# First weight rows in one tile, early sums in pairs of 64 columns, a shorter split, unit 3 transposed by TensorE, and a new order in an attention-and-MoE kernel

## The chip, the cores and the metric

The kernel runs on one core of a Trainium2 chip. The metric is the device time in microseconds (us), the median of three runs. The core has five engines with instruction streams of their own: PE (TensorE; the weight loads are shown apart as PEld), ACT (ScalarE), DVE (VectorE), POOL (GpSimd) and SP (SyncE, which here only issues DMAs). Each stream runs in the order in which it was written, and semaphores hold an instruction until what it needs is there.

## The reference

Attention over 4 batches, 8 heads, 768 positions and 64 values a head. Heads 0, 2 and 6 see all earlier positions; the other five see the last 64 positions and the first four (the sinks). Then a gated layer turns each of the 3072 tokens of 512 values into 2048 and back.

```
scores = where(mask, q @ k.T / 8, -1e9)              # per batch and head
a      = softmax(scores);  attn = a @ v
x      = attn, heads side by side                    # 3072 x 512
h      = x @ w_in                                    # 512 x 2048
out    = (h * sigmoid(beta * h)) @ w_out             # 2048 x 512
```

## The kernel before, in words

**Units.** The work is cut into eight units of 384 queries: unit n is half u = n % 2 of batch b = n // 2. Each goes through the same stages. q and k are loaded, cast to bf16 and turned, so that the head dimension lies on partitions (tiles `QK`). TensorE makes scores in rounds (`scores`, written S in what follows; unit, head pair, round), ACT takes their exponentials (`exps`, tile `es`), DVE multiplies by masks (`masks`). TensorE sums them per query and head (`sums`, `sums_d`) and multiplies them with v (`pv`, two halves). The reciprocals of the sums are spread over partitions, and the products with them are `xT`. The layer then takes 16 blocks of 128 columns of `w_in`: `mm1` is four matmuls of 384 columns, `swish_a` (ACT) a tanh into tile `t`, `swish_b` (DVE) the gate into `gT`. `mm2` multiplies `gT` with `w_out`: three output blocks of 16 matmuls, then a copy by ACT or DVE and a store.

**Early and late units.** Units 0 and 1 (`RD = 2`) have a way of their own: `sums` adds by matmuls with a column selector `esel`, 128 queries to a group of 32 partitions; `recips` takes reciprocals of 96x128; `split` cuts them into a high and a low bf16 part on other partitions of `hl` by one cast and three operations; `spread` is one matmul for each quarter of `xT`; `hold` copies pv's result out of PSUM, and `norm_held` multiplies. The later units send their sums through memory (`sums_turn`, `spread_w`, `spread_r`, all on SP's queue). Units below `TD = 3` are loaded by head pair (`load_qk`, 192 KB) and turned by TensorE (`transposes`, six 128x128 transposes for a head pair, then `qk_copy`); the others are loaded by blocks of 128 positions (`load_block`), cast on POOL and turned by three DMA transposes on SP's queue (`turn_block`).

**Weights.** `w_in` and `w_out` come in four transfers of 1 MB each into tile `wf`, of which there are three buffers. `cast_w_in` and `cast_w_out` cast them on POOL. The first 128 rows of `w_in` belong to heads 1 and 0, which `xT` holds in that order, so `swap_w_in` casts these rows by two instructions of 64 rows that change places.

**The order.** Nothing follows from loops. `add` (line 127 ff.) lists each step with its engine or a choice of engines, what it needs and gives, and which ring of buffers it takes from; `SEQUENCE` names the order of all 1104 steps and `CHOICE` the engine where there is a choice. Every engine gets its steps in the order of `SEQUENCE`. `fill` puts idle matmuls in front of unit 0's steps on PE. PSUM has four single banks (`b`) and two double ones (`sp`), so a score round waits until an earlier one has been read by ACT.

In the order of before, PE has these steps just ahead of the first mm1 of unit 0: unit 0's sums and pv, unit 1's S 3 0, unit 0's four spreads, unit 1's S 3 1, two transpositions, S 3 2 and S 1 0. SP issues q of unit 0 and part of unit 1 first, then v of unit 0, then weights; the four transfers of `w_out` are issued between 28 and 41 us, with the loads of q and k of unit 2 partly behind them. Unit 3's q and k are loaded at 45 to 55 us, and its three turns are issued at 60.6 us. The mm2 of unit 0 begins between mm1 blocks 7 and 8 of unit 1.

Of the kernel before, what the change touches and what calls it, by code (L numbers as in the profile page):

```python
# [8 lines left out]
F32 = mybir.dt.float32  # L9
BF16 = mybir.dt.bfloat16  # L10
# [14 lines left out]
TD = 3  # L25
# [65 lines left out]
]  # L91
CHOICE = (
    "addddddggggdaaaaaaadgddaagggggaddggddaaaaaaddaaddaaadddggagggdggagggadgdgaaaadagaadadaaaaddaaddadaaa"
    "aaada"
# [24 lines left out]
class _Plan:  # L119
# [10 lines left out]
    def add(self, eng, cost, f, needs=(), gives=(), take=(), drop=(), dma=0.0, mode=None, port=False, begun=()):  # L130
# [4 lines left out]
        self.ops.append((0, len(self.ops), dict(alts), (lambda e: f()) if one else f, tuple(needs), tuple(gives),  # L135
                         tuple(take), tuple(drop), dma, mode, port, tuple(begun)))

    def run(self):
# [4 lines left out]
        bus, lock = 2.0, 0.0  # L143
# [3 lines left out]
        for o in (self.ops[i] for i in SEQUENCE):  # L147
            _, i, costs, f, needs, gives, take, drop, dma, md, port, begun = o
# [22 lines left out]
            if dma:  # L171
                bus = max(bus, t + (0.5 if dma > 0.2 else cost)) + dma
                end = bus + (1.9 if dma > 0.2 else 3.2)
                now[e] = max(now[e], bus - 2.8)
# [15 lines left out]
def kernel(  # L190
# [27 lines left out]
    RINGS = dict(  # L218
        q2f=5, k2f=5, vf=3, wf=3, c=4, vb=2, vs=2, xT=2, gT=2, t=2, osb=3, R=1, sc=1, rec=1, hl=1, VE=2,
        KP1=1, KP2=1, KP3=1,  # L220
        sp=2, b=4, **{f"es{pi}_{u}": 1 for pi in range(NP) for u in range(2)})

# [1023 lines left out]
```

## Time and profile before

| what | value |
|---|---|
| median of 3 runs (lowest, highest) | 237.85 us (237.45, 237.98) |
| span of the profiled execution | 236.2 us (its own time is not listed apart; the median is 1.65 us above the span) |
| busy: PE, DVE, ACT, POOL | 224.1, 148.9, 145.3, 94.1 us |
| chain that ended last | PE 72%, DMA 18%, POOL 3%, the rest under 3% each |
| moved by DMA | 43.14 MB |
| granted TensorE clock | mean 0.978; half in the stretch from 13.0 to 23.3 us |

Nearly all lines of the program are recorded under one helper (L113), so the profile is read by tiles: `b<-xT,w_in` is mm1, `b<-w_out,gT` is mm2, `t` and `gT` are the two halves of the gate, `sp<-QK` are scores, `sp<-es,vb` is pv, `b<-ident,c` are transpositions by TensorE, `QK<-c` is a turn by DMA. Times in the timeline are from the first instruction; the second column is how long the group of merged rows lasted.

### The profile page before, as it was taken

The numbers are of one execution on the slowest core, as the hardware profiler recorded it, in microseconds if no ns is written. First come the engines' busy times: TensorE is split into PE (matmuls) and PEld (weight loads), VectorE is DVE, ScalarE is ACT, GpSimd is POOL, SyncE is SP. The second block draws the span as 40 slices with busy tenths as digits, with TensorE's granted clock in tenths as the row PEclk, the third lists the DMA queues.
The fourth block names the chain that finished last, engine by engine and source line by source line (L and its number), as shares of the span: only waits on it lengthen the run. The fifth ranks groups of instructions, "written<-read, shape, count | busy, mean of one in ns | idle before, by whom it ended". The sixth has DMA issues, their size and how long they took to land.

```text
span 236.2 us, 5989 instructions
## 1 busy us (share of the span) xinstructions
PE 224.1 (95%) x2337; PEld 128.3 (54%) x2359; DVE 148.9 (63%) x340; ACT 145.3 (62%) x247; POOL 94.1 (40%) x220
## 2 busy tenths in 40 slices
PE   8789889999999997999999999999999999999994
PEld 8447457555535454546556555655465554655553
DVE  4579699888736667397667557855478466344600
ACT  3889987866836457824996498247459452154720
POOL 5344787676265551596550238195212000000000
PEclk9965999999999999999999999999999999999999
DMA  6989999999999999999959899975570025210312
GB/s 196 312 203 375 346 260 318 319 269 230 184 213 231 222 219 195 199 157 287 223 144 200 127 262 223 189 132 126 130 175 3 2 92 142 89 44 3 133 44 89
DMA packets 91980, 43.14 MB, mean 183 GB/s; under 512 B 75808, under 2 KB 84720, under 8 KB 91952
## 3 DMA queue, kind: packets, MB, share of 16 engines
q1 hardware_dynamic: 90864, 41.98, 76.8%
q10 hardware_dynamic: 1088, 0.79, 1.1%
q8 instruction: 18, 0.29, 0.6%
q14 instruction: 10, 0.08, 0.1%
HBM read 32.38 MB, written 6.37 MB: 164 GB/s over the span
## 4 chain that ended last, share of the span: by engine, by line
PE 72%; DMA 18%; POOL 3%; SPq 2%; issue 2%; DVE 1%; ACT 0%; DVEq 0%; ACTq 0%
PE b L113 63%; PE sp L113 9%; DMA wf<-in_moe_w_out_dram 7%; DMA vf<-in_v_dram 7%; DMA q2f<-in_q_dram 2%; SPq L113 2%; DMA QK<-c 2%; POOL w_out L113 1%; POOL c L113 1%; DVE xT L113 1%; DVE c L113 0%; POOL vb L113 0%; ACT t L113 0%; DVE mask_s L113 0%; ACT osb L113 0%
## 5 line engine op out<-in xcount | busy, mean ns | idle before, releaser
L113 DVE SCALAR_TENSOR_TENSOR gT<-t,b 128x384 bf16<-128x384 f32 x128 | 69.2, 551 | 42.8 <-ACT t L113 39.0
L113 ACT ACTIVATE t<-b,beta_h 128x384 f32<-128x384 f32 x128 | 72.9, 583 | 36.1 <-PE b L113 30.2
L113 PE MATMUL b<-xT,w_in 128*128 128x384 bf16 x512 | 91.6, 326 | 0.9 <-DVE gT L113 0.6
L113 PE MATMUL b<-w_out,gT 128*128 128x512 bf16 (+1 forms) x378 | 87.7, 370 | 1.7 <-issue 1.0
L113 PEld LDWEIGHTS <-w_in 128*128 128x128 bf16 x512 | 48.6, 98 | 37.1 <-issue 2.5
L113 PEld LDWEIGHTS <-gT 128*128 128x128 bf16 x400 | 37.6, 98 | 39.2 <-issue 1.9
L113 ACT ACTIVATE es<-sp 128x768 bf16<-128x768 f32 (+3 forms) x64 | 49.1, 806 | 12.1 <-PE sp L113 11.8
L113 POOL CAST c<-wf 128x256 bf16<-128x256 f32 x60 | 22.6, 419 | 16.9 <-DMA wf<-in_k_dram 15.9
L113 ACT ACTIVATE osb<-b 128x512 f32<-128x512 f32 (+1 forms) x17 | 9.9, 585 | 25.9 <-PE b L113 20.0
L113 POOL COPY KP<-QK 128x64 bf16<-128x64 bf16 (+5 forms) x47 | 12.8, 320 | 27.8 <-DMA QK<-c 25.7
L113 PE MATMUL sp<-QK 64*64 64x64 bf16 (+6 forms) x402 | 19.8, 242 | 3.0 <-DMA QK<-c 1.2
L113 POOL CAST vb<-wf 128x512 bf16<-128x512 f32 x18 | 11.6, 667 | 16.2 <-DMA wf<-in_v_dram 16.2
L113 PEld LDWEIGHTS <-QK 64*64 64x64 bf16 (+1 forms) x402 | 10.4, 107 | 13.7 <-issue 11.5
L113 DVE TENSOR_TENSOR xT<-sp,R 128x768 bf16<-128x768 f32 (+3 forms) x18 | 11.6, 686 | 7.5 <-PE sp L113 7.4
L113 PE MATMUL sp<-es,vb 128*64 128x64 bf16 (+3 forms) x243 | 14.7, 245 | 0.0
L113 DVE TENSOR_TENSOR es<-es,mask_s 128x800 bf16<-128x800 bf16 (+5 forms) x24 | 13.1, 557 | 1.0 <-ACT es L113 1.0
L113 POOL COPY vs<-vb 64x1536 bf16<-64x1536 bf16 (+2 forms) x10 | 12.6, 1271 | 0.4
L113 PEld LDWEIGHTS <-vb 128*64 128x64 bf16 x243 | 12.4, 116 | 0.5
L113 DVE TENSOR_TENSOR es<-es,mask_c 128x256 bf16<-128x256 bf16 (+2 forms) x32 | 10.7, 348 | 2.7 <-ACT es L113 2.4
L113 POOL CAST w_in<-wf 128x384 bf16<-128x384 f32 (+1 forms) x20 | 10.1, 537 | 5.7 <-DMA wf<-in_moe_w_in_dram 5.4
L113 POOL CAST w_out<-wf 128x512 bf16<-128x512 f32 x16 | 10.1, 670 | 4.8 <-DMA wf<-in_moe_w_out_dram 4.8
L113 ACT COPY QK<-b 128x384 bf16<-128x384 bf16 (+1 forms) x16 | 8.3, 548 | 5.0 <-PE b L113 2.8
(92 smaller groups left out, 169.8 us busy)
## 6 DMA issues: line engine op xcount, KB each, us to landing
out_dram<-osb SPq DMA_DIRECT2D x23, 256.0 KB
wf<-in_v_dram SPq DMA_DIRECT2D x18, 256.0 KB
wf<-in_moe_w_in_dram SPq DMA_DIRECT2D x4, 1024.0 KB
wf<-in_moe_w_out_dram SPq DMA_DIRECT2D x4, 1024.0 KB
wf<-in_q_dram SPq DMA_DIRECT2D x15, 256.0 KB
wf<-in_k_dram SPq DMA_DIRECT2D x15, 256.0 KB
R<-rd SPq DMA_DIRECT2D x9, 384.0 KB
q2f<-in_q_dram SPq DMA_DIRECT2D x12, 192.0 KB
```

What stands on the lines that cost most here:

```text
L113: ins = f(*a, **k)
```

## The change

It has five parts and a new order.

- **First rows of w_in.** `load_w0` loads the first 128 rows into one tile, 64 rows by 1024 columns at a time, with the two halves of 64 rows already changed over. `cast_w0` casts 128x256 at a time, 8 times. `load_w_in` loads the other three blocks of 128 rows (768 KB instead of 1 MB). The `wf` ring keeps its three buffers and has five such tiles before `w_out` instead of four.
- **Sums of units 0 and 1.** They are cut into three parts, `SUMS = [(0,), (1, 2), (3,)]` by head pair, each issued when its pairs are ready. A matmul has 64 columns instead of 128, so there are twice as many (70 and 126 instead of 35 and 63), and the sums lie on 96x64 instead of 96x128.
- **Reciprocals and split.** The reciprocal is of 96x64; the split is a cast of 96x64, one operation of 96x64 and one bf16 product of 96x384.
- **Unit 3.** `TD = 4`: its q and k are loaded by head pair, cast by eight POOL instructions, and turned by 24 transposes of TensorE and four copies of 128x768 by ACT or DVE, instead of by blocks and three DMA transposes.
- **First mm1 blocks.** Blocks 0 and 1 of unit 0 are issued quarter by quarter, each quarter needing only its own part of `xT`.
- **Order.** `SEQUENCE` and `CHOICE` are new, and some of the costs that `add` is given. SP now issues unit 0's v right behind six loads of q and k; `w_out` comes behind all q and k of unit 2. PE's steps ahead of the first mm1 no longer hold unit 1's S 3 1, S 3 2, S 1 0 and three of its transpositions. All 32 mm1 blocks of units 0 and 1 come before the first mm2. Unit 4's three turns are issued before unit 3's sums go through memory; in the kernel before, two of them came behind.

```diff
-TD = 3
+TD = 4
...
-    def const_esel():
-        pool.memset(esel, 0.0)
-        for j in range(8):
-            pool.memset(esel[:, j, :, j:j + 1], 1.0)
+    def const_two():
+        pool.memset(two, 0.0)
+        pool.memset(two[:, 31:40:8], 1.0)
...
+    def load_w0(half, r):
+        if (half, r) == (0, 0):
+            wst["0"] = stg.tile([128, 2048], F32, name="wf", bufs=RINGS["wf"])
+        c = slice(half * d_ff // 2, (half + 1) * d_ff // 2)
+        sp.dma_start(out=wst["0"][r:r + D, c], in_=moe_w_in[D - r:2 * D - r, c])
...
-    def swap_w_in(s, half, eng):
-        f = wst["i", s][:, 0, half * FS:(half + 1) * FS]
-        for r in (0, D):
-            cast(eng, w_in_sb[2 * s + half][r:r + D, 0, :], f[D - r:2 * D - r, :])
+    def cast_w0(s, eng):
+        cast(eng, w_in_sb[s][:, 0, :], wst["0"][:, s * FS:(s + 1) * FS])
...
+    SUMS = [(0,), (1, 2), (3,)]
...
+            for s in range(2):
+                a = j * 128 + s * W
+                for h in heads:
+                    e8 = two[:, 31 - 16 * s - XH.index(h):63 - 16 * s - XH.index(h)]
...
+                    pe.matmul(x.sm[32 * j:32 * j + 32, 0:W], l, e, start=(part == r == 0),
+                              stop=(part == len(SUMS) - 1 and r == len(byj[j]) - 1))
...
-        dve.reciprocal(x.sm[0:96, 0:128], x.sm[0:96, 0:128])
+        dve.reciprocal(x.sm[0:96, 0:W], x.sm[0:96, 0:W])
...
-        for j in range(TU):
-            r = slice(32 * j, 32 * j + 32)
-            dve.scalar_tensor_tensor(out=hl[r, j * 128:(j + 1) * 128], in0=hi[r], scalar=low[r], in1=rec[r],
-                                     op0=MULT, op1=ADD)
+        dve.scalar_tensor_tensor(out=lo, in0=hi, scalar=low[0:96], in1=rec, op0=MULT, op1=ADD)
+        dve.tensor_mul(x.hl, lo.unsqueeze(1).to_broadcast([96, CK, W]), blk)
...
+        if n == 0 and s < 2:
+            for t in range(NP):
+                add("pe", 0.163, lambda t=t: mm1(x, s, [t]), needs=[("xT", n, t)] + ([("h", n, s, t - 1)] if t else needs if s != 1 else needs[:2] + [("h", n, 0, 0)]),
+                    gives=[("h", n, s, t)] + ([("h", n, s)] if t == NP - 1 else []), take=[] if t else take)
```

More of the change, by code (lines that the diff above doesn't have):

```diff
@@ L128, in __init__, with add @@
         self.same = {}
-    def add(self, eng, cost, f, needs=(), gives=(), take=(), drop=(), dma=0.0, mode=None, port=False, begun=()):
+    def add(self, eng, cost, f, needs=(), gives=(), take=(), drop=(), dma=0.0, mode=None, port=False, begun=(), lat=None):
         needs = dict.fromkeys(m for n in needs for m in self.same.get(n, [n]))
@@ L135, in add @@
         self.ops.append((0, len(self.ops), dict(alts), (lambda e: f()) if one else f, tuple(needs), tuple(gives),
-                         tuple(take), tuple(drop), dma, mode, port, tuple(begun)))
+                         tuple(take), tuple(drop), dma, mode, port, tuple(begun),
+                         lat or (1.9 if dma > 0.2 else 3.2)))
     def run(self):
@@ L147, in run @@
         for o in (self.ops[i] for i in SEQUENCE):
-            _, i, costs, f, needs, gives, take, drop, dma, md, port, begun = o
+            _, i, costs, f, needs, gives, take, drop, dma, md, port, begun, lat = o
             e = {"a": "act", "d": "dve", "g": "pool"}[choice[i]] if i in choice else list(costs)[0]
@@ L172, in run @@
                 bus = max(bus, t + (0.5 if dma > 0.2 else cost)) + dma
-                end = bus + (1.9 if dma > 0.2 else 3.2)
+                end = bus + lat
                 now[e] = max(now[e], bus - 2.8)
@@ L218 @@
     RINGS = dict(
-        q2f=5, k2f=5, vf=3, wf=3, c=4, vb=2, vs=2, xT=2, gT=2, t=2, osb=3, R=1, sc=1, rec=1, hl=1, VE=2,
+        q2f=5, k2f=5, vf=3, wf=3, c=4, vb=2, vs=2, xT=2, gT=2, t=2, osb=3, R=1, sc=1, rec=1, VE=2,
         KP1=1, KP2=1, KP3=1,
@@ L724, in sink_from, with sums @@
         return 2 * W if u == 0 else 0
-    def sums(x):
-        sm = bank((x.n, "s"))
-        if x.n == 0:
-            fill(sm[:, 0:128])
+    SUMS = [(0,), (1, 2), (3,)]
+    def sums(x, part):
+        if part == 0:
+            x.sm = bank((x.n, "s"))
+            if x.n == 0:
+                fill(x.sm[:, 0:128])
         byj = [[] for _ in range(TU)]
+        heads = [h for pi in SUMS[part] for h in PAIRS[pi]]
         for j in range(TU):
-            if j * 128 >= sink_from(x.u):
-                byj[j].append((esel_k.rearrange("p a b -> p (a b)"), x.esk[0:96, j * 128:(j + 1) * 128]))
-        for hpos, h in enumerate(XH):
-            e8 = esel[:, hpos, :, :].rearrange("p a b -> p (a b)")
-            for j in range(TU):
-                if RETR[h]:
-                    byj[j] += [(e8, e[:, j * 128 - q0:j * 128 - q0 + 128])
-                               for (kb, q0, n, e) in x.work[h] if q0 <= j * 128 < q0 + n]
-                else:
-                    byj[j].append((e8, x.work[h][:, j * 128:(j + 1) * 128]))
+            for s in range(2):
+                a = j * 128 + s * W
+                for h in heads:
+                    e8 = two[:, 31 - 16 * s - XH.index(h):63 - 16 * s - XH.index(h)]
+                    if RETR[h]:
+                        byj[j] += [(e8, e[:, a - q0:a - q0 + W]) for (kb, q0, n, e) in x.work[h] if q0 <= j * 128 < q0 + n]
+                    else:
+                        byj[j].append((e8, x.work[h][:, a:a + W]))
+                if part == len(SUMS) - 1 and a >= sink_from(x.u):
+                    byj[j].append((esel_k[:, 16 - 16 * s:48 - 16 * s], x.esk[0:96, a:a + W]))
         for r in range(max(len(w) for w in byj)):
@@ L745, in sums @@
                     l, e = byj[j][r]
-                    pe.matmul(sm[32 * j:32 * j + 32, 0:128], l, e, start=(r == 0), stop=(r == len(byj[j]) - 1))
-        x.sm = sm
+                    pe.matmul(x.sm[32 * j:32 * j + 32, 0:W], l, e, start=(part == r == 0),
+                              stop=(part == len(SUMS) - 1 and r == len(byj[j]) - 1))
     def sums_d(x):
@@ L899, in norm, with mm1 @@
         dve.tensor_mul(x.xT[0:D, 3, 256:NQ], o[D:128, 1, NQ:512], x.RX[D:128, :])
-    def mm1(x, fi):
-        if fi == 0:
+    def mm1(x, fi, parts=range(NP)):
+        if fi == 0 and 0 in parts:
             x.gT = gp.tile([128, FO, NQ], BF16, name="gT")
-        h = bank(("h", x.n, fi))
-        for pi in range(NP):
+        h = bank(("h", x.n, fi)) if 0 in parts else x.h[fi]
+        for pi in parts:
             pe.matmul(h[:, 0:NQ], w_in_sb[fi // FO2][:, pi, fi % FO2 * 128:(fi % FO2 + 1) * 128], x.xT[:, pi, :],
@@ L969, in attention @@
         b, u = x.b, x.u
+        first_half = n - u
+        was = [n - 4 + v for v in range(2 - u)] if n >= 4 else []
         for pi in range(NP if n < TD else 0):
@@ L991, in attention @@
                 add("sp", 1.28, lambda j=j: turn_block(x, j), dma=1.25,
-                    needs=[("c", n, 0, j), ("c", n, 1, j)] + [("sc", n - 4 + v, pi) for pi in range(NP) for v in range(2 - u) if n >= 4],
+                    needs=[("c", n, 0, j), ("c", n, 1, j)] + [("sc", v, pi) for pi in range(NP) for v in was],
                     gives=[("QKb", n, j)], drop=[("c", (n, j))])
@@ L995, in attention @@
         for j in range(TU):
-            if not b:
-                add("sp", 1.0, lambda j=j: load_v(x, j, sp), dma=1.22,
+            if n < 2:
+                add("sp", 1.0, lambda j=j: load_v(x, j, sp), dma=1.35,
                     gives=[("vf", n, j)], take=[("vf", (n, j), 1)])
@@ L1002, in attention @@
             add(("pool", "dve") if early else ("pool",), (0.58, 0.36), lambda e, j=j: cast_v(x, j, ENG[e]), port=True,
-                needs=[("vf", n, j)] + ([("v", n - u, 0)] if (u, j) != (0, 0) else []),
-                gives=[("v", n, j)], drop=[("wf" if b else "vf", (n, 0 if b else j))], take=[("vb", b, 4 if b else 5)] if (u, j) == (0, 0) else [])
+                needs=[("vf", n, j)] + ([("v", first_half, 0)] if (u, j) != (0, 0) else []),
+                gives=[("v", n, j)], drop=[("vf", (n, j)) if n < 2 else ("wf", (n, 0))], take=[("vb", b, 4 if b else 5)] if (u, j) == (0, 0) else [])
         add(("dve", "pool"), (1.2, 3.0), lambda e: shift_v(x, ENG[e]), port=True,
-            needs=[("v", n, j) for j in range(TU)] + ([("v", n - 1, TU - 1)] if u else []), gives=[("vs", n)], take=[("vs", n, 2)])
+            needs=[("v", n, j) for j in range(TU)] + ([("v", first_half, TU - 1)] if u else []), gives=[("vs", n)], take=[("vs", n, 2)])
         if n == 0:
-            add("pe", 0.23, lambda: sink_rows(b), needs=[("v", n, 0), ("const", "sink")], gives=[("VKp", b)],
+            add("pe", 0.3, lambda: sink_rows(b), needs=[("v", n, 0), ("const", "sink")], gives=[("VKp", b)],
                 take=[("b", (n, "k"), 1)], drop=[("vb", b), ("KP2", "c")])
-            add("dve", 0.6, lambda: sink_copy(b), needs=[("VKp", b)], gives=[("VK", b)],
+            add("dve", 0.55, lambda: sink_copy(b), needs=[("VKp", b)], gives=[("VK", b)],
                 take=[("VE", b, 4)], drop=[("b", (n, "k"))])
@@ L1019, in attention @@
                 gives=[("ve", b)], take=[("VE", b, 4)], drop=[("vf", ("e", b))])
-        vready = [("v", n, j) for j in range(TU)] + ([("vk", n), ("ve", b)] if b else [("vs", n), ("VK", b)])
+        vready = [("v", n, j) for j in range(TU)] + ([("vk", n), ("ve", b)] if n >= 2 else [("vs", n), ("VK", b)])
         if u:
-            vready += [("v", n - 1, j) for j in range(TU)]
+            vready += [("v", first_half, j) for j in range(TU)]
         for pi in range(NP if n < TD else 0):
-            wait = [("sc", n - 4 + j, pi) for j in range(2 - u) if n >= 4]
+            wait = [("sc", v, pi) for v in was]
             if early:
                 for i, nm in enumerate(("q2", "k2")):
-                    add("pe", 0.24, lambda pi=pi, i=i: transposes_of(x, pi, i), needs=[("c", n, pi, nm), ("const", "ident"), ("const", "fill")],
+                    add("pe", 0.2, lambda pi=pi, i=i: transposes_of(x, pi, i), needs=[("c", n, pi, nm), ("const", "ident"), ("const", "fill")],
                         gives=[("T", n, pi, i)], take=[("b", (n, "T", pi, i), 1)], drop=[("c", (n, pi))])
@@ L1043, in attention @@
             add(("pool", "dve"), (2.8, 1.15), lambda e: [kp_copy(x, pi, ENG[e]) for pi in kp], port=True,
-                needs=[("QK", n - v, pi, 1) for pi in kp for v in range(u + 1)] + [("KP", n - 1, pi) for pi in kp if n > 2],
+                needs=[("QK", v, pi, 1) for pi in kp for v in {n, first_half}] + [("KP", n - 1, pi) for pi in kp if n > 2],
                 gives=[("KP", n, pi) for pi in kp], take=[(f"KP{pi}", n, 1) for pi in kp])
@@ L1088, in attention @@
         M = [("M" if mask_cost(pi, ri, n) else "E", n, pi, ri) for (pi, ri) in rounds]
-        add("pe", ([1.7, 1.4] if n < RD else [0.58, 0.98])[u], lambda: (sums if n < RD else sums_d)(x), needs=M + ([("const", "esel"), ("const", "sink")] if n < RD else [("const", "one")]), gives=[("sum", n)],
-            take=[("b", (n, "s"), 1)], drop=[(f"es{pi}_{u}", n) for pi in range(NP)] + ([("KP1", "k")] if n == 1 else []), mode="sum")
         if n < RD:
-            add("dve", 0.88, lambda: recips(x), needs=[("sum", n)], gives=[("rec", n)])
-            add("dve", 1.3, lambda: split(x), needs=[("rec", n), ("const", "sel"), ("const", "zero")], gives=[("hl", n)],
-                take=[("hl", n, NP)], drop=[("b", (n, "s"))])
+            for part, pis in enumerate(SUMS):
+                final = part == len(SUMS) - 1
+                add("pe", [0.4, 0.5][u], lambda part=part: sums(x, part),
+                    needs=[m for m in M if m[2] in pis] + ([] if part else [("const", "two")]) + ([("const", "sink")] if final else []) +
+                    ([("sum", n, part - 1)] if part else []), gives=[("sum", n, part)] + ([("sum", n)] if final else []),
+                    take=[] if part else [("b", (n, "s"), 1)], drop=[(f"es{pi}_{u}", n) for pi in pis] + ([("KP1", "k")] if n == 1 and final else []), mode="sum")
+        else:
+            add("pe", [0.58, 0.98][u], lambda: sums_d(x), needs=M + [("const", "one")], gives=[("sum", n)],
+                take=[("b", (n, "s"), 1)], drop=[(f"es{pi}_{u}", n) for pi in range(NP)], mode="sum")
+        if n < RD:
+            add("dve", 0.5, lambda: recips(x), needs=[("sum", n)], gives=[("rec", n)])
+            add("dve", 0.9, lambda: split(x), port=True, needs=[("rec", n), ("const", "sel")], gives=[("hl", n)],
+                take=[("sc", ("hl", n), NP)], drop=[("b", (n, "s"))])
             for t in range(NP):
@@ L1098, in attention @@
                     needs=[("hl", n)] + ([("sb", n, 0)] if t else []), gives=[("sb", n, t)],
-                    take=[("b", (n, "R", t), 1)], drop=[("hl", n)])
+                    take=[("b", (n, "R", t), 1)], drop=[("sc", ("hl", n))])
                 add("dve", 0.47, lambda t=t: norm_held(x, t),
@@ L1132, in first @@
         drop = [("xT", n)] if s == FO - 1 else []
-        add("pe", 0.65, lambda: mm1(x, s), needs=[("xT", n, t) for t in range(NP)] + [("wi", s), ("w0", s // FO2)] +
-            ([("h", n, s - 1)] if s else []), gives=[("h", n, s)], take=take, drop=drop)
+        needs = [("wi", s), ("w0", s // FO2)] + ([("h", n, s - 1)] if s else [])
+        if n == 0 and s < 2:
+            for t in range(NP):
+                add("pe", 0.163, lambda t=t: mm1(x, s, [t]), needs=[("xT", n, t)] + ([("h", n, s, t - 1)] if t else needs if s != 1 else needs[:2] + [("h", n, 0, 0)]),
+                    gives=[("h", n, s, t)] + ([("h", n, s)] if t == NP - 1 else []), take=[] if t else take)
+        else:
+            add("pe", 0.65, lambda: mm1(x, s), needs=[("xT", n, t) for t in range(NP)] + needs, gives=[("h", n, s)], take=take, drop=drop)
         add("act", 0.48, lambda: swish_a(x, s), needs=[("h", n, s), ("beta",)], gives=[("t", n, s)], take=[("t", (n, s), 1)])
@@ L1181 @@
     add("pool", 1.8, const_masks, gives=[("const", "m")])
-    add("pool", 0.7, const_esel, gives=[("const", "esel")])
+    add("pool", 0.2, const_two, gives=[("const", "two")])
     for u in range(2):
@@ L1189 @@
     add("dve", 0.2, const_one, gives=[("const", "one")])
-    add("dve", 0.4, const_zero, gives=[("const", "zero")], take=[("KP3", "c", 2)])
+    add("dve", 0.15, const_zero, gives=[("const", "zero")], take=[("KP3", "c", 2)])
     add("dve", 1.55, const_sink, needs=[("const", "ident")], gives=[("const", "sink")], take=[("KP2", "c", 1)])
-    add("dve", 0.9, const_sel, needs=[("const", "ident")], gives=[("const", "sel")])
+    add("dve", 1.4, const_sel, needs=[("const", "ident")], gives=[("const", "sel")])
+    for half in range(2):
+        for r in (0, D):
+            first_one = (half, r) == (0, 0)
+            add("sp", 0.5, lambda half=half, r=r: load_w0(half, r), dma=0.72, gives=[("w0f", half, r)], begun=[("begun", "0")] if first_one else [],
+                needs=[] if first_one else [("begun", "0")], take=[("wf", "w0", NS)] if first_one else [])
+    for s in range(NS):
+        add(("pool", "dve", "act"), (0.36, 0.2, 0.33), lambda e, s=s: cast_w0(s, ENG[e]), port=True,
+            needs=[("w0f", s // 4, 0), ("w0f", s // 4, D)], gives=[("w0", s)], drop=[("wf", "w0")])
     for s in range(NS // 2):
         for w, ld, ca in (("i", load_w_in, cast_w_in), ("o", load_w_out, cast_w_out)):
-            add("sp", 0.5, lambda s=s, ld=ld: ld(s), dma=2.9, gives=[("wf", w, s)], begun=[("begun", w, s)],
-                take=[("wf", (w, s), 6 if w == "i" else 4)])
+            add("sp", 0.5, lambda s=s, ld=ld: ld(s), dma=2.9 if w == "o" else 2.2, gives=[("wf", w, s)], begun=[("begun", w, s)],
+                take=[("wf", (w, s), 4)])
             for i in range(4):
@@ L1199 @@
                     gives=[("w" + w, 4 * s + i)], drop=[("wf", (w, s))])
-            for half in range(2 if w == "i" else 0):
-                add(("pool", "dve", "act"), (0.7, 0.4, 0.7), lambda e, s=s, half=half: swap_w_in(s, half, ENG[e]), port=True,
-                    needs=[("wf", w, s)], gives=[("w0", 2 * s + half)], drop=[("wf", (w, s))])
     for n in range(N):
```

56 lines of the change are left out of this document (30 added, 26 removed), and 108 rows, old and new, of the table SEQUENCE.

## The prediction

> **What bounds the kernel now.** I read the page's busy rows first, then what PE waits for, then the timelines of ACT and DVE up to 42 us, last the chain. On the page:
>
> ```profile
> PE   8789889999999997999999999999999999999994
> ACT  3889987866836457824996498247459452154720
> PEclk9965999999999999999999999999999999999999
> DMA  6989999999999999999959899975570025210312
> ```
>
> A digit is 5.9 us. From the seventh on PE shows 9, but for one 7 at 89 to 94 us, and no other engine comes near that later. All that PE waits for:
>
> ```profile
> PE b L113 <- DVE xT L113: 1.4, 2, 1.1
> PE sp L113 <- DMA QK<-c: 1.2, 1, 1.2
> PE b L113 <- issue: 1.0, 6, 0.2
> PE b L113 <- ACT c L113: 0.9, 1, 0.9
> ```
>
> That is little. So the end is when PE first gets steady work, plus all its work from there. The first mm1 starts at 27.39 us, from 30.4 us PE hardly waits, its last matmul ends at 233.0 us, and a copy and a store take 3.2 us more. There are two levers: an earlier start, and fewer or shorter waits and steps on PE behind it. What sets the start is ACT:
>
> ```profile
> 6.17 0.86 ACT L113 COPY QK<-b 128x384 bf16<-128x384 bf16 x2 [1.98 <-DMA k2f<-in_k_dram]
> ...
> 20.42 1.65 ACT L113 CAST w_in<-wf 64x256 bf16<-64x256 f32 x4
> ...
> 26.94 1.52 ACT L113 ACTIVATE es<-sp 128x768 bf16<-128x768 f32 x2
> 28.33 0.60 ACT L113 ACTIVATE t<-b,beta_h 128x384 f32<-128x384 f32 x1
> ```
>
> From 6.17 to the first tanh at 28.33 ACT has 12 copies of 0.49, 15 exponentials of 0.81, 6 weight casts of 0.40, one cast of 0.51 and two holds of 0.80: 22.6 us in a stretch of 22.2 us. It has no gaps to speak of.
>
> **Part 1, the start.** In the new order ACT has ahead of the first tanh 8 copies (3.9), 12 exponentials (9.8), 3 casts of q and k (1.5), two holds (1.6) and two casts of the first rows, which I price like the 64x256 row, same columns, 0.40 each (0.8): 17.6 us, 5.0 less. DVE's side of the chain gets shorter too:
>
> ```profile
> 20.89 0.95 DVE L113 RECIPROCAL b<-b 96x128 f32<-96x128 f32 x1
> 21.87 0.29 DVE L113 CAST hi<-b 96x128 bf16<-96x128 f32 x1
> 22.19 1.05 DVE L113 SCALAR_TENSOR_TENSOR hl<-hi,low,b 32x128 bf16<-32x128 bf16 x3
> 23.83 1.95 DVE L113 TENSOR_TENSOR xT<-b,R 128x384 bf16<-128x384 f32 x4 [0.59 <-PE b L113]
> ```
>
> Half the columns make the reciprocal about 0.5. Cast and first operation are 0.2 to 0.3 each (rows of 0.28 and 0.34 for twice the columns), the 96x384 product 0.43 (row es x mask, 128x384). So 2.29 us become 1.4 to 1.5, and mm1 by quarters begins behind the first of four xT, not the last. That is worth nothing beyond ACT's 5.0, it only keeps DVE from being late in its stead: unit 0's v, landed at 14.6 to 16.6, is now issued about 5 us earlier (its issue took 4.6, and the loads of unit 1 that it passed come later by that; the transpositions that need them stand behind the first mm1 now). Two things eat into the 5.0: the last k load is issued by ACT behind its first copy, and score rounds wait for PSUM banks. I allow 0.8 (the one such load before cost POOL a wait of 1.95). The first tanh comes at 24.1, the first mm1 at **23.2**, 4.2 earlier.
>
> **Part 2, what was moved behind the start.** It still has to be done, so I follow PE to the end of unit 1's last mm1. PE's work is 32 blocks of 0.652 (four matmuls of 0.163 start to start) = 20.9; unit 1's other three transpositions 0.5, five score rounds 1.7, sums 1.7, pv 2.35, spread 0.7; unit 2's transposes 1.5 and two rounds 0.8. Sum 30.2, so 53.4 if PE is never kept waiting. The 126 matmuls of unit 1's sums are not in the trace: at 12 ns, like 64x64 scores (49 in 0.58), they take 1.5, at 23 ns, like the present ones (63 in 1.45), 2.9. I take 1.7, since the 64-column pv rows run at 15 ns. But between xT of unit 0 and pv of unit 1, DVE has 9 gates of 0.55, three QK copies 1.65, six masks of unit 1 and one constant 3.1, a cast of v 0.6, three other casts 1.2 and the shift of v 1.43:
>
> ```profile
> 36.50 1.43 DVE L113 COPY vs<-vb 64x1536 bf16<-64x1536 bf16 x2
> ```
>
> Sum 12.9, from 23.5 to 36.4, with some waits of its own 36.9. PE's work in that leg is 11.7 and ends at 34.9, so **PE waits 2.0 us for DVE**. pv ends at 39.3, the last xT at 43.5 (four of 0.49 with three gates between), PE waits 0.5 again. Then 16 blocks, three transpositions and two rounds, 12.4, end at 55.9; ACT, with 14 tanh of 0.58, two copies of 0.80 and two exponentials up to the bank that the last block needs, allows 55.8. I take **56.0**. The kernel before had, at 57.25, 27 such blocks and 16 mm2 (of 0.216); the new one has five blocks and one round more and 16 mm2 less, 3.7 against 3.5, so the equal point of before is 57.5. Gain 1.5 us.
>
> Costed at nothing, all under PE's work: 6 fewer SP issues and the three turns of unit 3 against 8 loads (14 us of SP's queue become about 4), four extra loads of w_in; 16 casts of 64x256 become 8; POOL's selector 0.77 becomes about 0.4; unit 3's 12 casts of 0.42 become 8 of 0.53; its four PSUM copies, 3.4 us of ACT and DVE at 56 to 70 us, where ACT is under half busy. Uncovered, that last would cost at most 3.4.
>
> **Part 3, behind it.** Unit 3's transposes are new work on PE. The nearest row is unit 2's:
>
> ```profile
> 54.01 0.50 PE L113 MATMUL b<-ident,c 128*128 128x128 bf16 x6
> 54.34 1.03 PE L113 MATMUL b<-w_out,gT 128*128 128x512 bf16 x4
> ```
>
> Six take 0.33 until mm2 goes on; the other twelve took 0.6 per six. So 1.3 to 2.4 for 24; I take 1.6. Against that, two waits should go. One is unit 4's turn:
>
> ```profile
> 89.36 3.76 DMA QK<-c
> 93.12 0.14 issue
> 93.26 0.50 PE sp L113 x6
> ```
>
> The chain runs through SP, whose two turns stood behind unit 3's sums; now they stand ahead (-1.2). The other is mm1 of unit 2 behind xT at 85 us (0.5, part of the 1.4 above): 12 mm2 now stand between pv and it instead of one. What is late next is unit 3's transposed q and k; their casts are due on POOL about 5 us ahead. Net gain 0.1 to 0.2.
>
> Sum: 1.5 + 0.2 = 1.7 us off a span of 236.2, so 234.5; with the 1.65 between the span and the median shown, **236.1 us**.
>
> A rule that speaks against part 3: the Trainium skill, "TensorE: Matmul & The Clock Gate", Part 4, says that a 128x128 transpose on TensorE takes about 275 ns in a kernel, most of it access latency. By that 24 would be 6.6 us, an estimate, and the sum 241.1. The trace does not bear it out as a price per transpose: each lasts 219 ns, but six start within 0.33.
>
> **Rivals.**
> *PE stays full.* DVE's 12.9 us has too few gaps filled in my count, or PE's order gives other work first; then PE ends mm1 at 53.4 instead of 56.0: 233.5. For it: before, PE hardly waited from 30.4 on with DVE at 88% in 27.4 to 52.5 us. Against: there mm2 stood between the blocks. 0.21.
> *The start is not earlier by much.* ACT's 5 us less are lost to waits for q and k (DMA at 9 tenths) and the clock, which is at half from 13.0 to 23.3 us and may fall in another stretch. If the first mm1 comes at 24.9, as late by 1.7 as the sum gains, nothing is won: 237.8. 0.13.
> *POOL's casts of w_out are late (slower).* POOL now has the copy KP of unit 2 (2.8) among them, and it needs the last transposition of unit 2. From there POOL needs 2.8 + 11 casts of 0.67 + 2 casts of 0.53 = 11.2, and PE gets to the first mm2 that needs the last cast (block 10) after 14 blocks, two rounds, six transposes and nine mm2, 12.4, less the copy between, 1.5. So there is no slack, and w_out comes behind five more loads of q and k (1 MB, 2.9 us at the 346 GB/s of the page's fifth slice).
>
> ```profile
> L113 POOL CAST w_out<-wf 128x512 bf16<-128x512 f32 x16 | 10.1, 670 | 4.8 <-DMA wf<-in_moe_w_out_dram 4.8
> ```
>
> If each cast took 1.0 beside a busy DVE (POOL's vs copies take 1.47 for DVE's 0.60), PE waits 3.6: 239.7. It turns slower than before from a wait of 1.7. 0.20. Against: four such casts ran in 2.30.
> *The transposes run one after the other*, 219 ns each: 24 make 5.3 instead of 1.6, 239.8. Six within 0.33 speak against it: 0.02.
>
> **How the numbers follow.** Forecast (235.0 to 237.3) 0.42, the rest as given; 0.02 for a reshuffled later order that costs PE over 2 us. A measurement tells 0.2%, 0.48 us, from no change. Faster: 0.42 + 0.21 = 0.63. Same: 0.13. Slower: 0.24. The range goes from the middle of the full-PE case with cheap sums (232.9) to just short of the POOL case (239.4).
>
> **What would show it.** First tanh near 24; ACT without gaps from 6 to 24; a wait of PE for DVE's vs or es near 35 to 37; no wait for QK<-c at 92; 24 more transposes within 1.3 to 2.4 us; the last mm1 of unit 1 near 56. I am wrong if PE waits for w_out at 56 to 60, or if the first tanh is past 26.

## The result and the profile after

The changed kernel takes 239.62 us (median of 15 runs, 238.01 to 241.43); the kernel before, run beside it, takes 237.54. The ratio is 1.0082, with a 95% interval of 1.0056 to 1.0109: **slower by 0.8%**, where 0.7% faster was forecast. The profiled execution took 240.27 us with a span of 238.6. Ratios, here and below, leave out executions over 1.5% above the fastest of their kernel, so they can differ a little from the quotient of the medians.

The forecast had three parts, and each can be read off the trace as a mark on PE:

| mark on PE (us) | before | forecast | after | k of pair 2 early (below) |
|---|---|---|---|---|
| first mm1 (part 1) | 27.39 | 23.2 | 26.00 | 21.26 |
| first mm2 behind all early mm1 (end of part 2) | 57.5, the equal point | 56.0 | 58.46 | 54.95 |
| last matmul ends (part 3) | 232.97 | 231.3 | 235.38 | 231.82 |

From mark to mark: part 1 came out 2.8 us late. Part 2 took 32.46 instead of 32.8 us, near the forecast. Part 3 took 176.9 instead of 175.3 and cost 1.6 more than forecast. Beside the kernel before, the first mm2 came 0.96 us behind the equal point and the last matmul 2.41 behind, so 1.45 us of the loss arose in part 3 and not at the start.

The same rows of the page as before (40 slices, here of 6.0 us):

```profile
PE   6499999999999999999999999999999999999994
ACT  2577995789435728835785049622957477018611
PEclk9955999999999999999999999999999999999999
DMA  6999999995978997999959795946850101901022
```

PE is at 9 from the third slice on, with no 7 at 90 us any more. But the first two slices are emptier than before (64 for 87), ACT has 257 where it had 388, and the clock is at half in the third and fourth slice. By windows of 3.4 us it was at 0.50 from 10.74 to 24.39 us, 13.65 us long, against 10.24 us in before. The record of the clock begins only at 3.91 us (6.20 in before), and the views count the time ahead of it as full. But the 128x128 matmuls there last 314 ns, as they do in the half stretch, and 219 between the two, so PE began at half clock: that makes 17.6 us of it in all, against 16.4. All that PE waits for:

```profile
PE b L115 <- POOL c L115: 3.0, 3, 1.8
PE b L115 <- issue: 2.0, 11, 0.4
PE sp L115 <- ACT QK L115: 1.4, 1, 1.4
PE b L115 <- DVE xT L115: 1.4, 2, 1.1
PE sp L115 <- DMA QK<-c: 0.5, 1, 0.5
PE b L115 <- ACT osb L115: 0.5, 1, 0.5
```

The 1.2 us for `QK<-c` at 92 us went. New are POOL's cast `c` and ACT's copy `osb`. The timeline of ACT, whose gaps stand in brackets, shows where the start was lost:

```profile
6.12 0.48 ACT L115 COPY QK<-b 128x384 bf16<-128x384 bf16 x1 [2.46 <-PE b L115]
7.61 0.37 ACTq L115 DMA_DIRECT2D k2f<-in_k_dram  x1
8.03 0.48 ACT L115 COPY QK<-b 128x384 bf16<-128x384 bf16 x1 [1.43 <-DMA k2f<-in_k_dram]
...
13.00 0.81 ACT L115 ACTIVATE es<-sp 128x768 bf16<-128x768 f32 x1 [1.87 <-PE sp L115]
...
27.52 1.13 ACT L115 ACTIVATE t<-b,beta_h 128x384 f32<-128x384 f32 x2
```

From 6.12 to the first tanh at 27.52 ACT waits eight times, 5.8 us in all. The first two belong to one load, that of k of unit 0's pair 2. The chain of what ended last runs straight through it:

```profile
2.84 4.75 DMA k2f<-in_k_dram
7.59 0.02 issue
7.61 3.72 DMA k2f<-in_k_dram
```

The load landed at 11.33, and POOL's cast, ready for it since 6.7, followed. The copy ahead of it ended at 6.60, but the load went out only at 7.61, 0.02 us after another load had landed. That other is SP's k of *unit 1*. The semaphores in the records of the two queues explain it (start, queue, tile, semaphore waited for, semaphore given):

```
0.801 ACT k2f   -     100        4.376 SP  q2f  100   100
0.805 SP  q2f   -     102        4.789 SP  vf   102   102
1.313 ACT k2f   -     104        5.476 SP  vf   104   104
...                              5.926 SP  vf   105   105
2.838 SP  k2f   -     109        7.612 ACT k2f  109   109
```

The build has eight completion semaphores for these loads and hands them out in turn. The ninth load, and those behind it in this list, wait until the load that held the same semaphore has landed, whatever it was. ACT's load got that of a load issued late. The Trainium skill, "DMA: Bandwidth & Descriptors", section "Why a DMA increments its semaphore by 16 and not by 1", gives a reason for such a wait: with two DMAs in flight on one semaphore, early completions of the second can fill the count that stands for the first.

DVE's leg came out as priced: 2.29 us before, 1.39 now, without a stall (between these rows lie the cast, 0.21, and the operation, 0.28):

```profile
20.55 0.55 DVE L115 RECIPROCAL b<-b 96x64 f32<-96x64 f32 x1
...
21.78 0.35 DVE L115 TENSOR_TENSOR sc<-lo,blk 96x384 bf16<-96x384 bf16 x1
```

### The profile page after: what moved, and what is told of

Its sections match the earlier page's. It is cut to its first block, busy times and chain, and to the rows that moved or that the text cites. A ratio compares the mean times of both kernels' runs of the same rounds, so it can differ in the third digit from the quotient of the medians.

```text
span 238.6 us, 6224 instructions
## 1 busy us (share of the span) xinstructions
PE 225.8 (95%) x2450; PEld 128.9 (54%) x2471; DVE 155.0 (65%) x351; ACT 139.6 (59%) x237; POOL 89.9 (38%) x203
## 4 chain that ended last, share of the span: by engine, by line
PE 78%; DMA 7%; ACT 5%; DVE 4%; SPq 3%; issue 2%; POOL 0%; DVEq 0%
PE b L115 67%; PE sp L115 11%; DMA k2f<-in_k_dram 4%; SPq L115 3%; ACT es L115 2%; DMA QK<-c 2%; DVE gT L115 1%; ACT t L115 1%; DMA out_dram<-osb 1%; DVE es L115 1%; ACT QK L115 1%; DVE vs L115 1%; ACT osb L115 0%; DVE sc L115 0%; ACT w_in L115 0%
## 5 line engine op out<-in xcount | busy, mean ns | idle before, releaser
L115 PE MATMUL b<-xT,w_in 128*128 128x384 bf16 x512 | 90.3, 326 | 0.8 <-ACT osb L115 0.5
L115 PE MATMUL b<-w_out,gT 128*128 128x512 bf16 (+1 forms) x379 | 85.3, 370 | 2.1 <-issue 1.6
L115 POOL CAST c<-wf 128x256 bf16<-128x256 f32 x48 | 19.4, 447 | 21.8 <-DMA wf<-in_q_dram 9.1
L115 ACT ACTIVATE osb<-b 128x512 f32<-128x512 f32 (+1 forms) x12 | 6.8, 564 | 25.2 <-PE b L115 24.8
L115 POOL COPY KP<-QK 128x64 bf16<-128x64 bf16 (+5 forms) x48 | 14.1, 342 | 14.7 <-DMA QK<-c 7.9
L115 DVE TENSOR_SCALAR osb<-b 128x512 f32<-128x512 f32 x13 | 8.9, 688 | 11.0 <-PE b L115 8.3
L115 POOL CAST vb<-wf 128x512 bf16<-128x512 f32 x18 | 11.1, 632 | 12.0 <-DMA wf<-in_v_dram 12.0
L115 DVE TENSOR_TENSOR es<-es,mask_c 128x256 bf16<-128x256 bf16 (+2 forms) x32 | 11.2, 368 | 5.6 <-ACT es L115 5.6
L115 POOL CAST w_in<-wf 128x384 bf16<-128x384 f32 (+1 forms) x18 | 9.6, 572 | 8.4 <-DMA wf<-in_moe_w_in_dram 6.0
L115 PE MATMUL b<-ident,c 128*128 128x128 bf16 x96 | 9.8, 234 | 3.0 <-POOL c L115 3.0
```

The lines of the kernel that those rows point to most:

```text
L115: ins = f(*a, **k)
```

## The experiments

Each kernel was run beside the kernel before on the same chip, so ratios are compared; the median of before lay between 237.8 and 238.1 us. Steps are named as in the program: `f` a load, `c` a cast, `T` a transposition (unit, pair).

**1. The one load, earlier** (k02_early). The changed kernel; in `SEQUENCE` one step moves ahead of ACT's first copy:

```diff
 act: f 0 0 k2, f 0 1 k2, f 0 3 k2
+act: f 0 2 k2
 act: QK 0 0 0
-act: f 0 2 k2
```

> The changed kernel with one step moved: ACT issues the load of k of unit 0's pair 2 right behind its other three, ahead of its first copy, instead of behind it. Theory A (the start was lost to this load): in the changed kernel it was issued at 7.61 us, landed at 11.38, and ACT then stood idle for 1.87 us; here it lands by about 8, the first tanh comes near 25.6 instead of 27.5, and the whole span gets about 1.5 to 2 us shorter, level with the kernel before. Theory B (what counts is the work and the engines behind the first mm1): the first tanh may come earlier, but unit 1's last mm1 still ends near 58.4 and the span moves by less than 0.5 us.

235.72 us (234.73 to 236.70), ratio **0.9918 [0.9889, 0.9948]**. From 1.0082 to 0.9918 is 1.6%, 3.9 us, for one step of 1131.

```profile
0.80 2.07 ACTq L118 DMA_DIRECT2D k2f<-in_k_dram  x4
...
10.74 0.81 ACT L118 ACTIVATE es<-sp 128x768 bf16<-128x768 f32 x1 [0.33 <-PE sp L118]
```

The four loads go out together, the gap of 1.87 ahead of the third exponential is 0.33, and ACT's gaps from 6.27 to the first tanh at 22.80 sum to 1.07. The granted clock stays at 1.0 from 9.94 us on. So moving this one load gains more than the change had lost, and twice the 1.5 to 2 us that were expected. The half stretch from 10.74 to 24.39 us went with it, so this run doesn't tell the load's own part from the clock's. That 0.8% faster comes close to the 0.7% forecast is luck: against the forecast the first mm1 is 1.9 us early (21.26 for 23.2), part 2 takes 0.9 more (33.69 for 32.8) and part 3 1.6 more (176.87 for 175.3).

**2. Is it the place, or the clock?** (warm_fill, k02_warm.) Idle matmuls are added ahead of unit 0's steps to keep PE busy through the gap, 62 of them in the changed kernel and 48 in k02_early:

```diff
-    def fill(dst):
-        for _ in range(int(held["gap"] / 0.14)):
+    def fill(dst, more=0):
+        for _ in range(int(held["gap"] / 0.14) + more):
```

> The changed kernel with more idle matmuls on PE where it waits anyway between 7 and 12 us (20 ahead of unit 0's first scores, 6 and 4 ahead of the next two, 6 and 26 ahead of the transpositions of pair 2). Theory A2 (the start was lost to the clock, which was at half from 10.74 to 24.39 us): the granted clock stays at 1.0 there, unit 0's sums, pv and spreads take half the PE time, the first tanh comes 1 to 2 us earlier, the span 1 to 2 us shorter. Theory B: the clock may stay up, the span moves by less than 0.5 us, since ACT and DVE set the pace. If the clock falls anyway, the test says nothing on either.

> Both of the edits before: the early load of k and more idle matmuls (12 instead of 26 ahead of pair 2's second transposition). Theory A and A2 together: first tanh near 24 to 24.5, as the prediction had it, and a span 2.5 to 3.5 us below the changed kernel's, below the kernel before by 0.5 to 1. Theory B: unit 1's last mm1 at about 58 whatever the start is, under 0.5 us gained.

warm_fill: 239.58, ratio 1.0073 [1.0041, 1.0106]; k02_warm: 238.45, ratio 1.0029 [0.9993, 1.0064]. In both the clock stayed at 1.0 from about 9 us on. The first mm1 of warm_fill came at 24.28 instead of 26.00 and its profiled span is 1.2 us shorter, but its median time is that of the changed kernel. k02_warm shows the price of the fills: they run past the moment when the scores could start (first exponential at 10.03 us with a gap of 1.71; in k02_early at 8.41), and the kernel loses 1.1% to k02_early. These fills are no clean test of the clock, and they are no remedy.

**3. The load in its place, its semaphore free** (k10_late). The changed kernel; only SP's load of k of *unit 1* moves, behind its q and the first load of v, so that ACT's load takes over a semaphore that comes free earlier:

```diff
-sp: f 1 0 k2, f 1 0 q2, vf 0 0
+sp: f 1 0 q2, vf 0 0, f 1 0 k2
```

> The changed kernel with ACT's load of k of unit 0's pair 2 where it stands, behind ACT's first copy, but SP's load of k of unit 1's pair 0 moved behind its q and the first load of v. In the build the loads share eight completion semaphores in turn; ACT's load took over that of SP's load, which was issued at 2.84 and landed at 7.59, and went out at 7.61. Now it takes over one whose load lands before 6. If that wait is what held it, it goes out right behind the copy, at 6.6 to 6.7, 1 us earlier, and lands by 10.4; the first mm1 then comes 1.0 us earlier than 26.00 and the time is 238.4 to 238.8, or 236.5 to 237.5 if the half clock goes with it. Rival: the transfers ahead of it in the DMA engines set its landing, not its issue: it lands at 11.0 to 11.5 and the time stays at 239.3 to 239.9.

237.34 us, ratio 0.9983 [0.9948, 1.0017].

```profile
6.31 0.37 ACTq L118 DMA_DIRECT2D k2f<-in_k_dram  x1
...
11.85 0.81 ACT L118 ACTIVATE es<-sp 128x768 bf16<-128x768 f32 x1 [1.51 <-PE sp L118]
```

The load goes out at 6.31 instead of 7.61 and lands 4.21 us later, at 10.52 instead of 11.33. The first mm1 comes at 23.41, 2.6 us earlier, and the ratio falls by 1.0%. The load itself gained only 0.8; in this run the half stretch in the clock's record was 3.41 us long (12.06 to 15.48) instead of 13.65. The rival (the engines set the landing, not the issue) named a landing at 11.0 or later and is out by that, but the engines have a part: of the 1.3 us gained at the issue, 0.5 went into the longer time to landing (4.21 for 3.72). What the later load for unit 1 does by itself was not tested. So the 1.6% of the first experiment divide into about 1.0% for the semaphore and 0.65% for the place behind the copy, that move's part and the clock's included.

**4. The same step in the kernel before** (before_k3). ACT's fourth load of k, issued at 5.76 us in before, moves ahead in the same way.

```diff
-act: f 0 0 k2, f 0 2 k2, f 0 1 k2, c 0 0 q2, f 0 3 k2
+act: f 0 0 k2, f 0 2 k2, f 0 1 k2, f 0 3 k2, c 0 0 q2
```

> The kernel before with ACT's fourth load of k (unit 0's pair 3) issued right behind its other three, ahead of its first cast, as k02_early does in the changed order. In before it was issued at 5.76 us, behind a wait for the semaphore of an earlier load that it takes over, and ACT then waited 1.98 us and POOL 1.95 us for k loads. Theory (where a late k load stands, the whole start is as much later): the first mm1 comes 1 to 2 us earlier than 27.39, and the time is 236.0 to 236.9. Rival: in before ACT's own work is the bound of the start and takes up the wait in other places: within 0.4 us of 237.5. If it gains 2 us, most of what k02_early gained over before is this load and not the change.

238.57 us, ratio 1.0000 [0.9962, 1.0038]. The first mm1 came 0.67 us earlier in the trace, which the times don't show. The time lies where the rival had it. Its reason, that ACT's work fills the whole start and covers an earlier load, is argued and not tested. So k02_early's gain over before belongs to the change and not to this load alone.

**5. No fills at all** (k02_nofill). k02_early with `range(0)` in `fill`; only idle matmuls are left out.

> k02_early with no idle matmuls at all (the fills ahead of unit 0's steps are left out; they add nothing to the result). It completes a square: k late and half clock (the changed kernel, first mm1 26.00), k late and full clock (warm_fill, 24.28), k early and full clock (k02_early, 21.26). If PE's granted clock falls to half somewhere between 8 and 25 us, and the clock is a cost of its own, the first mm1 comes 1.5 to 3 us later than 21.26 and the time is 237.0 to 238.7. Rival: with k early the start is set by ACT's work, and a PE at half speed is still in time: first mm1 within 0.5 us of 21.26, time within 0.5 us of 235.7. If the clock doesn't fall although nothing fills PE's gaps, the fills are not what holds it.

238.90 us (236.84 to 239.89), ratio 1.0042 [1.0011, 1.0074], so 1.2% slower than k02_early. But its profiled execution was the fastest of its twelve (236.84) and had its first mm1 at 20.64. It ran at half clock until the clock's record begins at 10.60 us, and at full clock from there, as the durations of its transposes show (lowest, median and highest in ns):

```profile
L118 PE MATMUL b<-ident,c x24: 286/314/314, 4.7 to 9.5; 128*128 128x128 bf16 x24
...
L118 PE MATMUL b<-ident,c x21: 217/219/246, 10.5 to 24.6; 128*128 128x128 bf16 x21
```

The fills are worth about 3 us in the usual execution. That this is the clock isn't shown: the six executions with a mean clock of 0.998 or more have a median of 238.43, the six at 0.991 to 0.993 one of 238.97, and the mean counts what lies ahead of the record as full.

**6. Unit 3's transposes in the order of before** (before_td4). `TD = 4` in the kernel before; the loads, casts, transposes and copies of unit 3 stand near the places of the old steps.

```diff
-TD = 3
+TD = 4
```

> The kernel before with unit 3's q and k loaded by pairs and turned by TensorE (four head pairs, one copy on DVE, three on ACT), in the order of before, the transposes among the mm2 of unit 0 at 64 to 69 us. Theory P (new work on PE counts in full): 1.3 to 1.6 us longer than before, less the 1.2 us wait for a turn at 92 us if that goes. Theory Q (it frees SP's queue and the DMAs enough): the wait at 92 goes and the span is level or up to 1 us shorter.

240.35 us, ratio 1.0131 [1.0086, 1.0177]. The 24 transposes took 2.57 us of PE from start to start. Of this, 0.89 is a wait for one of the PSUM copies, which I had costed at nothing:

```profile
62.11 0.81 PE L117 MATMUL b<-xT,w_in 128*128 128x384 bf16 x4 [0.89 <-ACT QK L117]
```

By the first mm1 of unit 2 the kernel is 2.2 us late (87.10 for 84.93), more than the 1.3 to 1.6 expected; the wait for `QK<-c` at 94 is still there, at 0.5 instead of 1.2. This part of the change pays only with an order made for it.

**7. The price of a transpose** (k02_again, k02_t3x3). k02_early again as the base, and with unit 3's transposes done three times in place:

```diff
-                pe.transpose(x.ps[pi][:, i, t, :], ...
+                for _ in range(3 if x.n == 3 else 1):
+                    pe.transpose(x.ps[pi][:, i, t, :], ...
```

> k02_early once more, as the base for the next run on the same chip: 235.4 to 236.2 us and a ratio of 0.989 to 0.995 to before.

> k02_early with each of unit 3's 24 transposes by TensorE done three times in place (48 more; the result stays the same). If a transpose costs its slot of 55 to 60 ns from start to start, 48 cost 2.6 to 2.9 us, less what falls into waits: 1.8 to 3.0 us above k02_again, and the 24 that the change adds cost 1.3 to 1.5. Rival: each costs what it lasts, 219 ns: 10.5 us more; by the figure of the Trainium skill, "TensorE: Matmul & The Clock Gate", Part 4 (about 275 ns), 13 us, an estimate. Second rival: PE has slack at that place and they cost nothing: within 0.6 us of k02_again.

k02_again: 235.31, ratio 0.9916 [0.9886, 0.9947]. k02_t3x3: 237.25, ratio 0.9988 [0.9962, 1.0014]. The 48 added transposes cost 1.94 us, **about 40 ns each** (the two intervals leave some 20 ns either way), and the stretch behind the first mm2 is longer by 1.86 in the trace. That is less than the 55 to 60 expected. Both rivals are out. The Trainium skill's 275 ns ("TensorE: Matmul & The Clock Gate", Part 4) is no price per transpose where several follow each other.

**8. The store that took the place of the turn** (k02_store). In the changed kernel PE waits at 92 us again, now for ACT's copy of an output block:

```profile
89.98 2.29 DMA out_dram<-osb
92.27 0.02 issue
92.29 0.61 ACT osb L115
```

The copy waits for a buffer, the buffer for its store, and the store stood in SP's queue behind unit 4's turns, the very steps that had been moved ahead. In k02_early it is moved back ahead of the last two:

```diff
+sp: store osb 0 1
 sp: QKb 4 0, QKb 4 2, sum_t 3
-sp: store osb 0 1
```

> k02_early with one store of unit 0's output moved on SP's queue: it is ready when unit 4's turns begin and is now issued ahead of the last two of them, instead of behind them and behind unit 3's sums (issued at 85.27 us in k02_again, landed at 87.56; TensorE then waited 1.08 us for ACT's copy into that buffer; 0.41 us in k02_early, 0.50 in the changed kernel). Theory: in the new order unit 4's turns no longer stand behind unit 3's sums, and TensorE's wait of 1.20 us for QK<-c went, but the store that now stands behind them brought a new one. Then the wait goes, and the time is 0.4 to 1.1 us below k02_again's 235.31 and k02_early's 235.72: 234.4 to 235.2, ratio to before 0.984 to 0.990. Rival: the turns behind the store come later by what its issue takes, and TensorE waits for QK<-c again: no gain, ratio 0.990 to 0.994.

235.91 us, ratio 0.9903 [0.9871, 0.9936]. In the trace the theory holds: the wait (1.08 in k02_again) is gone, the turns bring none back, and the stretch from the first mm2 to the end is 175.80 us, where k02_early has 176.87 and k02_again 176.88. The time doesn't show it: the interval takes in k02_early's ratio, and the start of the profiled execution was 0.4 later. Nor can the whole 1.07 us be this wait: in k02_early it was only 0.41, and the stretch there is as long as in k02_again with 1.08. That the wait goes is shown; a gain is not.

**9. The first rows earlier** (k02_w0, w0_store). In k02_early PE waits 1.07 us at 30.45 for the cast of the first rows; their last two loads move ahead of w_in's third transfer. w0_store has this and the store.

```diff
+sp: w0f 1 0, w0f 1 64
 sp: wf i 2
-sp: w0f 1 0, w0f 1 64
```

> The changed kernel with the load of k of unit 0's pair 2 early, as in k02_early, and besides with the last two loads of the first rows of w_in (256 KB each) issued ahead of the third 768 KB transfer of w_in instead of behind it. In k02_early TensorE waits 1.07 us at 30.45 us for the cast of those rows, which waits 1.29 us for its load. If PE is what sets the time from the first mm1 on, most of this wait goes: 0.5 to 1.0 us below k02_early's 235.72, so 234.7 to 235.2. Rival: VectorE's work between unit 0's xT and unit 1's pv is due next at the same point, or the third transfer of w_in is late instead: within 0.3 us of 235.7.

> The same with the two loads of the first rows ahead of w_in's third transfer as well (k02_w0): the attempt at the best of these. By the theory 0.4 to 1.1 us below k02_w0's 0.9929, so a ratio of 0.986 to 0.992; between the two kernels of this call no difference over 0.6 us.

k02_w0: 235.97, ratio 0.9929 [0.9893, 0.9964]; w0_store: 235.99, ratio 0.9911 [0.9882, 0.9939]. The wait fell to 0.2 in both, but in both new waits for a cast of q by ACT (0.8) and for DVE's gates (0.6) came in its place. The times lie where the rival had them: no gain. None of these kernels is measurably better than k02_early, the best version found.

## Why the prediction was wrong, point by point

**The step that failed is in part 1:** "the last k load is issued by ACT behind its first copy, and score rounds wait for PSUM banks. I allow 0.8". The risk was named and priced from the one such load in before, which cost POOL 1.95. Here POOL waited 4.66 for it, and ACT 5.8 in all, 3.3 of it for this load. From 11.95 to 24.44 the chain of what ended last is PE's work alone, at half clock. The prediction's own sign of being wrong, a first tanh past 26, came: 27.52. The price in before was low for a reason that I didn't look for: that load took over a semaphore that came free at 5.76, 1.85 us earlier than here. k02_early and k10_late show both halves of what I missed. The first tanh came 3.4 late: 5.0 more waits, less 1.6 because ACT's instructions overlap a little and its own work took 15.6 us instead of 17.2. In k02_early ACT waits 1.07, near the 0.8 allowed.

**The clock.** The rival "the start is not earlier by much" named it and had the right direction, at 0.13. The half stretch grew from 10.24 to 13.65 us, and ACT's last six gaps (2.5 us, all for PE) lie in it. In two other kernels, among the executions that the ratios take in, those that show more half clock are the longer ones: k10_late took 239.43 at a mean clock of 0.971, and 236.43 to 238.22 at 0.991 and above; k02_warm took 239.95 and 240.12 at 0.993, and 236.85 to 239.03 at 1.000. The changed kernel's own executions don't show it: the median is 239.62 for the five at 0.971 to 0.978 and 239.65 for the ten at 0.999 and above, and the mean counts the time ahead of the record as full. So how much of the loss is the late load itself, and how much the half clock that came with it, stays open. What pulls the clock down isn't settled either. In each of the five traces in which it falls during the start, PE was busy 1.50 to 2.32 of the 3.41 us just before, with no gap over 1.81 us, but windows with 2.02 to 2.26 were also followed by none.

**Part 2 was right in its sum, by luck.** PE was to work 30.2 us and to wait 2.5 for DVE. In the trace it stands idle for 0.8 us of the 32.46, 0.31 of them for DVE's xT, and its work takes 31.7 from start to start, mm1 alone 21.6 instead of 20.9. Unit 1's 126 sums took 2.25 us instead of 1.7 (0.43 of it a wait), and the shift of v ended 12.9 behind the first mm1 where 13.7 was forecast. So DVE's leg had about its length, but PE, with more work ahead of the same point, came to it hardly early.

**Part 3 was wrong by 1.6.** The transposes were right:

```profile
60.98 0.51 PE L115 MATMUL b<-ident,c 128*128 128x128 bf16 x6
```

The first six took 0.34 until mm2 went on, all 24 took 1.36 (forecast 1.6), and both waits named did go. But I asked "what is late next" only of unit 3's q and k. It was the store behind the turns (0.5 here, 1.08 in k02_again), and a later turn (`QK<-c`, 0.5 at 165 us). The remaining 0.6 is not assigned to a cause, and k02_early, where PE doesn't wait at 165 us, takes as long from its first mm2 to the end (176.87).

**The rivals.** POOL's casts of w_out were not late: eleven took 6.22 us, 0.57 each and not 1.0, and the last ended at 59.93 without a wait of PE. "PE stays full" had the waits nearly right, but with PE's longer work its time for part 2, 30.2 us, didn't come. The sum of the three errors, 2.8 − 0.3 + 1.6, is the 4.1 us by which the last matmul came later than forecast.

## What to carry to other kernels

Follow each early load back to its issue, and each issue to what it waits for: a DMA may wait for a semaphore held by a transfer that has nothing to do with it, and the cost of that shows on an engine two steps away. When a step is moved ahead in a queue, list what it now stands in front of, the stores too, and price the first of these that someone waits for. A part that is cheap in one order, such as unit 3's transposes, can cost 1.3% in another, so price it where it will stand. Check each wait of a forecast in the trace and not only the sum: in part 2 two errors hid each other.

## What the runs showed of the hardware

- By the packets in the trace of the changed kernel, loads of 64 partitions with 4096 B packets took 264 ns a packet. Packets of 2048 B started in the same stretches (14.7 to 20.2 and 24.9 to 28.3 us) took 104 ns: 15.5 against 19.6 GB/s for one DMA engine. The first rows of w_in, split into four such loads, came more slowly per byte. Whether the packet's size or the 64 partitions do it was not tested.
- The half clock came and went in steps of 3.41 us, and lasted on although PE was busy throughout its last three windows. This is one of them; the columns after its length are PE and the weight loads, then DVE, ACT and POOL, the granted clock and the DMA share:

```profile
17.56:20.98 3.42, 3.42 (x61) 1.96 (x60) 3.30 (x7) 3.02 (x6) 2.48 (x5) 0.50 1.02 256
```

The Trainium skill, "TensorE: Matmul & The Clock Gate", "Why this matters for your kernels", advises at least 4 us of continuous work on TensorE to get to the full clock. Here the clock came back only behind three such windows, 10.24 us (14.15 to 24.39). The profile's ends of matmuls are modelled, so PE may have idled in them unseen.
- A clock of 1.00 at the start of a trace need not be one: in all 14 traces the 128x128 matmuls ahead of the first entry of the clock's record last about 314 ns and those behind it 219. So PE ran at half up to 3.91 us in the changed kernel and up to 10.60 in k02_nofill.
